# Fused attention and feed-forward: one more block product a span in two levels of Strassen, and the attention's last multiply at the end of its run

## The chip, the cores and the metric

The kernel runs on one core of a Trainium2 chip. The metric is the device time of one execution in microseconds (us); the time of a kernel is the median of several executions. The core's engines are PE (matrix multiply; PEld is its weight load), DVE (vector), ACT (scalar and activation functions), POOL (the general engine) and SP, whose queue issues most of the DMAs here. Each engine takes its instructions strictly in the order in which the program wrote them, so work that waits on one engine holds back everything written behind it on that engine.

## The reference, cut to what matters

```python
batch, n_heads, seq, head_dim = (8, 12, 448, 64)
n_tokens, d_model, d_ff = (3584, 768, 2048)

q_n, k_n = (rmsnorm(q, g_q), rmsnorm(k, g_k))
scores = np.matmul(q_n, k_n.transpose(0, 1, 3, 2)) / np.sqrt(head_dim)
attn = np.exp(scores - np.max(scores, axis=-1, keepdims=True))
attn = attn / (np.sum(attn, axis=-1, keepdims=True) + 1e-09)
x = np.matmul(attn, v)            # then (B,H,S,D) -> (B*S, H*D)

h = x @ w_in                      # 3584 x 768 by 768 x 2048
g = np.maximum(h, 0.0) ** 2
out = g @ w_out                   # 3584 x 2048 by 2048 x 768
```

All is in float32. An x column is scaled by one over the sum of its exponentials; the kernel keeps the sum apart from the product with v and multiplies at the end. These are the "factors" of this text.

## The kernel before

The eight batches are taken two at a time, in four spans. A span holds 2 x 448 tokens and 12 head pairs (two heads side by side fill 128 partitions). Two batches side by side are what makes both feed-forward products 2 x 2 block problems, and each of these is done with Strassen's method in Winograd's form, seven block products in place of eight, named A11, A12, S1, S2, S3, A22, S4 after the weight block or sum that each takes. The weights' blocks and sums are worked out once, in the first stretch of the program, and stored in DRAM (`w1s`, `w2s`), from which they stream through five buffers (`sw`).

The order of the work is written out by hand. First the attention of span 0 alone (`attention_alone`). Then for each span: its first product (`first_product`: x by w_in, ReLU, square, and the differences of g that the second product needs), and then its second product (`second_product`: g by w_out) woven into the attention of the next span (`attention`). The last span's second product is done by `last_product`, which the change does not touch.

**The weaving.** `attention(first)` is a generator that stops (`yield`) five times a head pair, 66 times in all, and between two stops the main loop (L1497 to L1500) takes some steps of `second_product`, one step being one matmul of a filling product (PE runs it as two instructions). The attention of a head pair leaves at its first stop one solid block on PE (scores of the chunks 0 and 1, values of the pair before, scores of the chunks 3 and 2), and then PE has only filling until the next pair's block.

**A head pair on the other engines.** ACT: exponentials (L794), a copy of half of the values (L1004), four small copies for the norm (L748), the scaling of the transposed q (L769), the squares for the pair after next (L738), three small copies of the folded sums (L827). DVE: the sums of exponentials (L817, L815), the norm's reduction (L745) and arithmetic (L755, L756), transposes of the next pair (L768), the join of the two halves of the values (L910), x times its factors (L912), the folding of the sums (L824) and the factors themselves (L834 to L836). POOL: the power of -1/2 (L757), the norm's multiplies (L759), the combinations of x for the first product's Strassen sums in the second batch of a span (L922 to L927), a small DMA of the factors to DRAM (L1031), and two DMAs (L842) that read them back spread over 64 partitions each, straight into x's place, where L912 multiplies.

**The second product.** `FIRST[span]` of the seven block products are done in one level, as filling: three blocks of 8 matmuls of 448 columns each, every block evicted by DVE (L1195, L1197) or ACT (L1192), and those that complete an output are transposed on DVE (L1257) and stored by four DMAs (L1260). The others come after, in two levels: of their three row blocks, two are split again (28 matmuls of 224 columns for the parts pa, pb, pc, pd), and the third is done as before (`ps`, L1219). Their weights come as a set of four quarters (`load_set`, L1138), POOL adds up the weight sums (L1150, L1151, L1211, L1212), and DVE the sums of g (`add_g`, L1145). Which dead parts of the big buffers gT and gC hold the sets, the sums and the outputs is written out at the head of `second_product`. In the attention beside span 0's second product DVE also has the differences of g to do (`combine`, L1043 to L1047), as span 0's first product does not do them.

`FIRST` is (6, 5, 5): one product in two levels in span 0, two each in spans 1 and 2.

Of the kernel before, what the change touches and what calls it, by code (L numbers as in the profile page):

```python
# [387 lines left out]
def attention_then_ffn_bounded(  # L388
# [258 lines left out]
    FIRST = (6,5,5)  # L647
    order2 = (A11, A12, S2, S1, S3, A22, S4)
    plan, begins = [], {}
    for span in range(NSPAN):  # L650
# [3 lines left out]
        if span + 1 < NSPAN:  # L654
            plan += [(w2s[i, k, :, :, m * P:(m + 1) * P], 2 * NFC) for o, i in enumerate(order2)
                     for m in range(HC) if o < FIRST[span] or m == HC - 1 for k in range(HF // 4)]

# [232 lines left out]

    def finish(i):

        b, hp = divmod(i, NPAIR)
        pav, factors = pavs.pop(i), xT[:, b % 2, hp]
        x = factors
        if i < NAT:

# [10 lines left out]
        else:  # L908
            rest = rests.pop(i)
            nc.vector.tensor_tensor(rest, pav, rest, ALU.add)  # L910
            pav = rest
# [72 lines left out]
    def attention(first):  # L984
# [3 lines left out]
        for i in range(first, last + 1):  # L988
# [30 lines left out]
            if i > first:  # L1019
                finish(i - 1)  # L1020
# [5 lines left out]
            if i > first:  # L1026
                combine_x(i - 1)
            yield
            if i < last:
                factors_of(i)  # L1030
                nc.gpsimd.dma_start(sums["out"][i % 2], sums["square"][0:2 * S // 32, 1])  # L1031
                spread(i)
            yield
# [72 lines left out]
    def second_product(work, span):  # L1106
# [3 lines left out]
                  A12: gT[:, HF:, 0:S], A22: gC[:, 2], S4: gT[:, HF:, S:2 * S]}  # L1110
        HK, HS, NB = HF // 2, S // 2, HF // 2 * P
# [3 lines left out]
        first, end = FIRST[span], len(order2)  # L1115
# [3 lines left out]
        zone = {end - k: gC[:, k - 1].rearrange("p f n -> p (f n)") for k in (1, 2)}  # L1119
        tiles = {o: [z[:, k * NB:(k + 1) * NB].rearrange("p (c m) -> p c m", c=HK) for k in range(6)]  # L1120
                 for o, z in zone.items()}
        p1s = [work.tile([P, S], F32, tag="p1", name="p1", bufs=HC) for _ in range(HC)]
        ys = [work.tile([P, S], F32, tag="y", name="y", bufs=1)] + [zone[end - k][:, 6 * NB:6 * NB + S] for k in (2, 1)]
        spared = [gT[:, f, S:2 * S] for f in range(HF)]
        squares_of = [gT[:, HF + k, 0:S].rearrange("p (g n) -> p g n", n=32) for k in range(5)]

        def t_of(o, k):
            rows = gT[:, o % 2 * HF + 2 * k:o % 2 * HF + 2 * k + 2, 0:S]
            return rows.rearrange("p r (h n) -> p r h n", h=2)

        def parts_of(o):
            rhs = rhs_of[order2[o]]
            return [[rhs[:, k * HK:(k + 1) * HK, t * HS:(t + 1) * HS] for t in range(2)] for k in range(2)]

        def load_set(o):
            if o < end:
                for k, (m, h) in enumerate(((0, 0), (0, 1), (1, 0), (1, 1))):
                    nc.sync.dma_start(tiles[o][k], w2s[order2[o], h, :, :, m * P:(m + 1) * P])  # L1138
# [14 lines left out]
        def send(o):  # L1153
            for k in range(len(late)):
# [453 lines left out]
```

## Time and profile before

| | us |
|---|---|
| three executions: median (lowest, highest) | 1349.33 (1349.3, 1349.94) |
| the profiled execution, its own time | 1347.0 |
| its span, first to last instruction | 1345.2 |

| stage (us from the span's start) | length | DVE busy | ACT busy | POOL busy |
|---|---|---|---|---|
| 262.0 to 436.0, attention beside span 0's second product | 174.0 | 140.91 | 77.49 | 102.77 |
| 436.0 to 456.0, its two-level product | 20.0 | 8.61 | 0.56 | 8.38 |
| 581.5 to 737.0, attention beside span 1's second product | 155.5 | 119.98 | 75.85 | 101.80 |
| 737.0 to 776.0, its two two-level products | 39.0 | 20.52 | 1.36 | 18.23 |
| 900.0 to 1055.0, attention beside span 2's second product | 155.0 | 119.79 | 75.69 | 101.82 |

PE is busy in all of these from end to end, and the granted clock is 1.00 in each. A time of a kernel is that of the whole execution; the span is a little shorter, since something lies ahead of the first and behind the last recorded instruction. In rows of the profile "line engine op, out<-in" stands for a group of instructions or for a single one; in a timeline a row begins with the start and the length, and a bracket at its end says how long the engine had been idle before and which instruction's end let it go.

### The profile page before, as it was taken

To read this page: it belongs to the slowest core of one execution; us is meant where nothing else is said; L and a number is where in the kernel's file an instruction comes from. 1 tells how busy PE (TensorE), PEld (TensorE's weight loads), DVE (VectorE), ACT (ScalarE), POOL (GpSimd) and SP (SyncE) were. 2 spreads that over 40 slices of the span, in tenths; PEclk is the share of its full clock that TensorE was granted. 3 is DMA by queue.
4 is the path that set the end of the run, shared out by engine and by line. 5 is a ranking of instruction groups with operands and counts; after the bars stand their busy time and mean duration, and the time that the engine had idled before them with its cause. 6 is when DMAs were issued, how large, how long until landed. Compare 5 with 4: busy or idle time off the path is not lost.

```text
span 1345.2 us, 17641 instructions
## 1 busy us (share of the span) xinstructions
PE 1324.3 (98%) x5906; PEld 694.3 (52%) x5906; DVE 841.6 (63%) x1325; ACT 485.4 (36%) x938; POOL 664.2 (49%) x539
## 2 busy tenths in 40 slices
PE   8999999999999999999999999999999999999997
PEld 3333445444444655444444755444444665556887
DVE  6999788589777333467877523357777723336553
ACT  7886466544543011345553011235554101111000
POOL 5766533466574322647675412447676522322452
PEclk9999999999999999999999999999999999999999
DMA  8967999655666333345757333345664534421433
GB/s 226 249 210 201 315 361 328 186 130 118 132 131 157 90 88 88 98 109 125 152 128 168 79 96 88 91 114 118 128 130 125 127 89 135 133 87 50 115 102 58
DMA packets 413818, 190.19 MB, mean 141 GB/s; under 512 B 282388, under 2 KB 408724, under 8 KB 413716
## 3 DMA queue, kind: packets, MB, share of 16 engines
q1 hardware_dynamic: 406164, 180.21, 51.4%
q0 software_dynamic: 4736, 8.40, 2.4%
q8 instruction: 49, 0.80, 0.2%
q10 hardware_dynamic: 2816, 0.34, 0.2%
q14 instruction: 53, 0.43, 0.1%
HBM read 155.72 MB, written 33.16 MB: 140 GB/s over the span
## 4 chain that ended last, share of the span: by engine, by line
PE 87%; DVE 7%; ACT 3%; issue 1%; DMA 0%; SPq 0%; POOL 0%; ACTq 0%; DVEq 0%
PE ps L1175 21%; PE pd L1083 11%; PE pa L1083 10%; PE pc L1083 10%; PE sc L792 7%; PE pav L874 6%; PE pb L1083 5%; PE ps L1352 3%; PE ps L1219 2%; PE pd L1324 2%; PE pa L1324 2%; PE pc L1324 2%; ACT gT L804 1%; DVE gT L817 1%; PE pc L1160 1%
## 5 line engine op out<-in xcount | busy, mean ns | idle before, releaser
L757 POOL TENSOR_TENSOR half<-half,mhalf 128x28 f32<-128x28 f32 x36 | 184.5, 5125 | 83.6 <-DVE half L756 73.2
L1059 POOL TENSOR_TENSOR gT<-gT 128x448 f32<-128x448 f32 x96 | 93.8, 978 | 258.5 <-ACT gT L1055 258.5
L1175 PE MATMUL ps<-gT,sw 128*128 128x448 f32 x432 | 169.3, 545 | 0.0
L1055 ACT ACTIVATE gT<-gT 128x448 f32<-128x448 f32 x96 | 55.4, 577 | 300.1 <-DVE gT L1098 297.8
L1083 PE MATMUL pa<-xT,sw 128*128 128x448 f32 x384 | 155.0, 540 | 0.6 <-ACT p L1087 0.6
L1175 PE MATMUL ps<-gC,sw 128*128 128x448 f32 x336 | 131.4, 545 | 0.0
L1175 PEld LDWEIGHTS ps<-gT,sw 128*128 128x128 f32 x432 | 80.1, 190 | 87.5 <-issue 85.5
L792 PE MATMUL sc<-qkT 64*64 64x448 f32 (+1 forms) x1152 | 110.3, 497 | 0.3 <-ACT pr L794 0.2
L1083 PEld LDWEIGHTS pa<-xT,sw 128*128 128x128 f32 x384 | 72.7, 190 | 71.6 <-issue 70.3
L583 POOL TENSOR_TENSOR gC<-gC 128x384 f32<-128x384 f32 x64 | 76.4, 1211 | 63.1 <-DVE gC L579 61.4
L1175 PEld LDWEIGHTS ps<-gC,sw 128*128 128x128 f32 x336 | 62.4, 190 | 68.1 <-issue 66.1
L794 ACT ACTIVATE pr<-sc 128x896 f32<-128x896 f32 x87 | 76.8, 908 | 11.7 <-PE sc L792 11.7
L1098 DVE TENSOR_TENSOR gT<-z,pd 128x448 f32<-128x448 f32 x32 | 19.8, 619 | 97.7 <-PE pd L1083 82.0
L842 POOL DMA_DIRECT2D xT<-factors x72 | 38.0, 532 | 84.1 <-DMA factors<-square 60.0
L1083 PE MATMUL pd<-xT,sw 128*128 128x448 f32 x192 | 77.9, 542 | 1.5 <-DVE z L1090 1.3
L1083 PE MATMUL pd<-xC,sw 128*128 128x448 f32 x192 | 77.5, 540 | 0.7 <-DVE gT L1098 0.7
L1083 PE MATMUL pb<-xC,sw 128*128 128x448 f32 x192 | 77.5, 540 | 0.1
L1083 PE MATMUL pc<-xC,sw 128*128 128x448 f32 x192 | 77.4, 539 | 0.0
L1083 PE MATMUL pc<-xT,sw 128*128 128x448 f32 x192 | 77.4, 539 | 0.0
L874 PE MATMUL rest<-pr,vt 64*64 64x448 f32 x348 | 72.7, 537 | 0.0
L874 PE MATMUL pav<-pr,vt 64*64 64x448 f32 x348 | 72.7, 537 | 0.0
L759 POOL TENSOR_TENSOR qk<-qk,half 128x448 f32<-128x448 f32 x72 | 69.9, 991 | 2.8
(276 smaller groups left out, 2387.8 us busy)
## 6 DMA issues: line engine op xcount, KB each, us to landing
sw<-w1s SPq DMA_DIRECT2D x224, 192.0 KB, 2.4
sw<-w2s SPq DMA_DIRECT2D x106, 256.0 KB, 3.5
w1s<-gC SPq DMA_DIRECT2D x8, 1344.0 KB, 6.9
w2s<-gC SPq DMA_DIRECT2D x8, 1344.0 KB, 6.1
qk<-in_q_dram SPq DMA_DIRECT2D x144, 56.0 KB, 2.6
qk<-in_k_dram SPq DMA_DIRECT2D x144, 56.0 KB, 2.5
xT<-factors POOLq DMA_DIRECT2D x72, 112.0 KB, 3.6
out_dram<-osb SPq DMA_DIRECT2D x124, 56.0 KB, 1.9
```

Source lines behind the costliest of these rows:

```text
L583: nc.gpsimd.tensor_tensor(*[blocks_of(n)[:, place_of(n, i)] for i in (dst, x, y)], op)
L757: nc.gpsimd.tensor_tensor(half, half, mhalf, ALU.pow)
L759: nc.gpsimd.tensor_tensor(qkn[:, s], raw[:, s], half[:, s * NG:(s + 1) * NG].rearrange("p g -> p g ()").to_broadcast([P, NG, 32]), ALU.mult)
L792: nc.tensor.matmul(sc[part, h, 0:n], qkT[rows, 0, 1, keys], qkT[rows, 0, 0, of], start=True, stop=True)
L794: nc.scalar.activation(pr, sc[:, :, 0:n], AF.Exp)
L874: nc.tensor.matmul(into, vs[i][rows, h, c, :], probs[i, c][rows, h, :], start=(c == 0), stop=(c == NF), skip_group_check=True)
L1055: nc.scalar.activation(g, src, AF.Relu)
L1059: nc.gpsimd.tensor_tensor(g, g, g, ALU.mult)
L1083: nc.tensor.matmul(ps, stream[n + at][:, c], rhs[:, c], start=first and c == 0, stop=c == HC - 1, skip_group_check=not first)
L1175: nc.tensor.matmul(ps, stream[n][:, c % 4], rhs_of[i][:, c], start=c == 0, stop=c == HF - 1)
L1324: nc.tensor.matmul(ps, lhs[:, c], rhs[:, c], start=first and c == 0, stop=c == HK - 1, skip_group_check=not first)
L1352: nc.tensor.matmul(ps, weights_of(o, m, c // HK)[:, c % HK], rhs_of[i][:, c, part], start=c == 0, stop=c == HF - 1)
```

## The change

`FIRST` becomes (5, 4, 4): two products in two levels in span 0, three each in spans 1 and 2. Where it is 4, the order of the seven products is another one, so that A12 falls among the three, and S2 plus S1's running sums get tiles of their own (`zs`) beside `p1s`.

In the attention, the old `finish` is cut in two. `join` (the addition of the two halves of the values, which frees their PSUM bank) stays in its place; the multiply with the factors, and behind it `combine_x`, move to the end of the pair's run, behind the two DMAs of the next factors.

In span 0 the differences of g are spread over more of the filling. The four sums of g for the first two-level product are done one at a time, a block apart; each later set of weights is loaded one product ahead, and the weight sums for it are added later in the product. The sets, sums and outputs of the two-level products have new places, among them the attention's tiles of exponentials. The line-order change in the main loop moves only where the generator object is made.

```diff
-    FIRST = (6,5,5)
-    order2 = (A11, A12, S2, S1, S3, A22, S4)
+    FIRST = (5,4,4)
+
+    def order2(span):
+
+        return (A11, S2, S1, S3, A12, A22, S4) if FIRST[span] == 4 else (A11, A12, S2, S1, S3, A22, S4)
...
+    def join(i):
+
+        rest = rests[i]
+        nc.vector.tensor_tensor(rest, pavs.pop(i), rest, ALU.add)
+
     def finish(i):
...
         else:
-            rest = rests.pop(i)
-            nc.vector.tensor_tensor(rest, pav, rest, ALU.add)
-            pav = rest
+            pav = rests.pop(i)
         nc.vector.tensor_tensor(x, pav, factors, ALU.mult)
...
             if i > first:
-                finish(i - 1)
+                join(i - 1)
             if i + 3 < last:
                 squares(i + 3)
             yield
             if i < last:
                 fold(i)
-            if i > first:
-                combine_x(i - 1)
             yield
             if i < last:
                 factors_of(i)
                 nc.gpsimd.dma_start(sums["out"][i % 2], sums["square"][0:2 * S // 32, 1])
                 spread(i)
+            if i > first:
+                finish(i - 1)
+                combine_x(i - 1)
             yield
...
-        zone = {end - k: gC[:, k - 1].rearrange("p f n -> p (f n)") for k in (1, 2)}
-        tiles = {o: [z[:, k * NB:(k + 1) * NB].rearrange("p (c m) -> p c m", c=HK) for k in range(6)]
-                 for o, z in zone.items()}
...
+        zone = [gC[:, k].rearrange("p f n -> p (f n)") for k in range(2)]
+        tiles = {o: [zone[(first + 1 - o) % 2][:, k * NB:(k + 1) * NB].rearrange("p (c m) -> p c m", c=HK)
+                     for k in range(6)] for o in range(first, end)}
+        b11, b21, b12 = ([gT[:, r + f, at:at + S] for f in range(HF)] for r, at in ((0, 0), (HF, 0), (0, S)))
+        apart = first == 4
+        exps = [pr[:, h] for pr in places[:NJ] for h in range(2)]
+        homes = {first: exps, first + 1: b21 if apart else b12, first + 2: b12}
...
-                        if span == 0 and at < 8 * HF and at % 4 == 1:
-                            combine(at // 4 % HF, (at // 4 // HF,))
+                        if span == 0 and at < 6 * HF and at % 6 == 1:
+                            combine(at // 6, (0,))
+                        if span == 0 and 6 * HF <= at < 11 * HF and at % 5 == 4:
+                            combine(at // 5 - 9, (1,))
                         if c == 3:
-                            send(o)
-                        if o == first - 1 and c == 5:
-                            if m < 2:
-                                load_set(first + m)
-                            for k in ((0, 1), (2,), (3,))[m]:
-                                add_g(first, k)
-                            if m == 2:
+                            send()
+                        ahead = (o - first + 1) * HC + m + 1
+                        if ahead >= 0 and c == 5:
+                            if ahead == 1:
+                                load_set(first)
+                            add_g(first, ahead)
+                            if ahead == HC:
                                 add_weights(first)
...
             for k in range(3):
                 add_g(o + 1, k)
-            send(o)
+            send()
+            load_set(o + 1)
             ps = bank("ps")
...
             nc.vector.tensor_tensor(y, z, pc, add)
-            add_weights(o + 1)
-            deliver(work, span, third, HC - 1 + where[0], where[1],
-                    osb=rows_of[3].rearrange("p (g n) -> p g n", n=32))
+            deliver(work, span, third, HC - 1 + col, t, osb=home[4].rearrange("p (g n) -> p g n", n=32))
...
             nc.vector.tensor_tensor(into[1][:, left], into[1][:, left], pd, add)
+            add_weights(o + 1)
```

## The prediction

> **What bounds the kernel now.** I read the page first (engines, then the chain that ended last), then the chain in order of time, then the timelines of PE, DVE, ACT and POOL around one attention pair.
>
> ```profile
> PE 1324.3 (98%) x5906; PEld 694.3 (52%) x5906; DVE 841.6 (63%) x1325; ACT 485.4 (36%) x938; POOL 664.2 (49%) x539
> PE 87%; DVE 7%; ACT 3%; issue 1%; DMA 0%; SPq 0%; POOL 0%; ACTq 0%; DVEq 0%
> ```
>
> PE is busy throughout and carries the chain. So the first thing to ask of the change is how much less PE streams. The chain at the end of span 1's attention gives the price of a two-level product and of a block of a one-level one, and an earlier piece gives the place of one attention pair (the stretch of filling matmuls between two blocks of scores and values):
>
> ```profile
> 651.15 6.96 PE ps L1175 x18
> ...
> 742.21 1.51 PE pa L1160 x8
> 743.72 6.01 PE ps L1219 x16
> ...
> 758.81 1.51 PE pa L1160 x8
> ```
>
> A full block (16 instructions) takes 6.01 us, so a one-level product of three blocks takes 18.03. A two-level product takes 758.81 - 742.21 = 16.60. In between PE never stops, so PE alone sets that pace.
>
> Next I looked for what holds PE when it does stop. There is one clear place, in span 0, where the ACT and the PE timelines read
>
> ```profile
> 335.36 0.69 ACT L827 COPY quarters<-quarters 32x28 f32<-32x28 f32 x3 [2.77 <-DVE quarters L824]
> ```
>
> ```profile
> 337.70 0.98 PE L792 MATMUL sc<-qkT 64*64 64x448 f32 x8 [0.19 <-ACT pr L794]
> ```
>
> ACT works in order. Its small copies of DVE's column sums (L827, for pair i) stand ahead of the exponentials of pair i+1, and PE needs those to free the two score banks. The block of scores there began at 332.47 and the next filling at 338.61: 6.14 us, against 5.43 for an undisturbed block (683.57 to 689.00). So 0.71 us were lost because L827 began 2.89 us after the block did. The allowance is therefore 2.89 - 0.71 = 2.18 us after a block's start. What leads to L827 is DVE's row of work for a pair, here the pair whose filling began at 651.15:
>
> ```profile
> 651.31 1.16 DVE L768 STREAM_TRANSPOSE qkT<-qk 128x448 f32<-128x448 f32 x2
> 653.58 0.19 DVE L755 TENSOR_TENSOR half<-half,other 128x28 f32<-128x28 f32 x1 [1.11 <-ACT other L748]
> 653.80 0.18 DVE L756 TENSOR_SCALAR half<-half 128x28 f32<-128x28 f32 x1
> 653.98 0.65 DVE L1257 STREAM_TRANSPOSE osb<-ct 128x448 f32<-128x448 f32 x1
> 654.55 1.05 DVE L817 TENSOR_TENSOR acc<-acc,qkT 128x896 f32<-128x896 f32 x1
> 655.63 1.27 DVE L815 TENSOR_TENSOR acc<-acc,half 64x448 f32<-64x448 f32 x2
> 656.93 0.62 DVE L910 TENSOR_TENSOR half<-pav,half 128x448 f32<-128x448 f32 x1
> 657.59 0.62 DVE L912 TENSOR_TENSOR xT<-half,xT 128x448 f32<-128x448 f32 x1
> 658.13 1.10 DVE L824 TRANSPOSE_TENSOR_REDUCE quarters<-acc 128x28 f32<-128x896 f32 x1
> ```
>
> L824 ends 8.08 us after the filling began, though the block started at 658.11: only 1 us of allowance is left. And POOL, for the same pair, works round a loop of its own:
>
> ```profile
> 654.13 4.82 POOL L757 TENSOR_TENSOR half<-half,mhalf 128x28 f32<-128x28 f32 x1 [1.06 <-DVE half L756]
> 659.03 1.84 POOL L759 TENSOR_TENSOR qk<-qk,half 128x448 f32<-128x448 f32 x2
> 661.27 0.60 POOL L1031 DMA_DIRECT2D factors<-square  x1 [0.39 <-DVE square L836]
> 665.26 1.05 POOL L842 DMA_DIRECT2D xT<-factors  x2 [3.40 <-DMA factors<-square]
> ```
>
> It stands still between its two DMAs until the first has landed.
>
> **The sum, on PE.** Three products change from 18.03 to 16.60 us: 3 x 1.43 = 4.29 us less. That is the whole of what the change can give by doing less.
>
> **What is taken from under the attention.** Spans 1 and 2 now fill twelve pairs with 4 x 24 - 6 = 90 matmul steps where there were 114, spread over 61 turns, five a pair: 7.38 steps of 0.751 us (6.01 / 8) = 5.54 us a pair instead of 7.02. The pair's period, 12.62 us in span 1 (fillings begin at 600.84 and, ten pairs on, at 726.99), becomes 11.14. Span 0 goes from 14.2 to 12.62. DVE, ACT and POOL have the same attention to do in that shorter time.
>
> **DVE's row, spans 1 and 2.** L755 starts 2.43 us after the filling begins, since it waits for ACT's copies behind the exponentials, and this stays. From there: 0.40 to the end of L756, 1.08 (L817), 1.30 (L815), 0.66 (L910), 1.10 (L824): 6.97. The change takes L912 out of this row (0.54, and its wait for the spread DMA: 13.5 us in 13 places over the kernel), and the output transpose L1257 (0.57) is in no pair before S3. With 0.1 for the semaphore L827 starts at 7.07; the allowance is 5.54 + 2.18 = 7.72 (7 or 8 steps: 7.44 to 8.19). Margin 0.65. Into it come the evictions that the filling puts between (L1195, 0.56: S2's and S1's, about one in five pairs of the twelve, 0 to 0.2 lost each, 0.3 in all), and in one pair a g-sum of the second level as well (L1145, 1.05 to 1.91): 7.07 + 0.56 + 1.25 = 8.88 against 8.19, 0.7 lost. I take 1.0 a span. Bounds: 0 if the evictions fall into DVE's wait for ACT's copies, 3.8 if POOL sets the pace (below).
>
> **POOL's loop.** Its nine rounds in span 1 (592.10 to 703.90, without its waits for DVE and ACT) add up to 103.6 us, 11.5 each; in span 2 to 102.4. Against 11.14 it falls 0.36 us behind per pair, 3.2 us by the tenth, or 2.2 since PE's own loss of 1.0 gives it time. In the pair above the normalised tile was ready at 660.87 and its transpose started at 663.68, 2.8 us of reserve; the shorter period takes 1.48, and the 1.3 us by which L768 may slip before L755 is late come to it: 2.6. So it just holds, by 0.4 us.
>
> **Span 0.** The subtractions L1043 to L1047 (0.63 to 0.76 each) were two every 4 steps, and are now two every 6 and then every 5, one such pair of them inside DVE's row: 7.07 + 1.3 + an eviction of 0.56 to 1.13 = 8.9 to 9.5, against 7.02 + 2.18 = 9.2 (8.9 to 9.7). Four or five pairs lose 0 to 0.5: 1.6 us, where 0.71 was lost before. Net 0.9; bounds -0.7 and 2.5.
>
> **Into the first two-level product.** POOL's weight sums (L1150, L1151) stand behind the last run's spread and now behind three x combinations too (L925 to L927), which before ran while POOL waited. From the end of L836: 0.55 + 2.0 + 1.05, then 4.2, 2.65 and 1.35 (L1211): 11.8. L836 ends about 8.5 us after the last filling began, so a11 is ready at 20.3; PE wants it after 5.54 + 2.79 (values) + 4.51 (six steps) + 7.52 (pa and third block) = 20.4. I take 0.2 for each of spans 1 and 2, bounds 0 and 1.5; span 0 has 1.5 us more filling and costs nothing.
>
> **What I cost at nothing.** The tile set of the second and third two-level product is loaded one product ahead, behind 4 or 8 output DMAs on SP's queue (0.48 each) and their transposes: it starts 9 us into a product, needs 2.65 to issue and 4.7 to land (gC<-w2s), 14.3 of 16.6; if late, the next pa waits, 1 us each. Separate S2+S1 sums (zs), new homes for the outputs and the moved sums of g add no instruction. The exponential of the half chunk (L794) now waits for the later L912, 9.3 us after the filling began at the earliest, and its scores come at 10.5; behind it stand the exponential of chunk 2 and L1004.
>
> [...] L1145 took from 1.04 to 2.15 us for one and the same shape, and POOL's L925 1.13 or 1.92. [...]
>
> **Sum.** 4.29 - 0.9 (span 0) - 2.0 (two attention runs) - 0.4 (two entries) = 1.0 us. The profiled execution would go from a span of 1345.2 (1347.0 with what lies around it) to 1344.2 (1346.0). The median shown, 1349.33, is 2.33 above it, so 1348.3.
>
> **Rivals.** *The loops hold everywhere:* L912's waits were what made DVE late, and no pair loses PE time. For it: PE does not stop in spans 1 and 2 now. Against: 0.65 us of margin. Then 4.29 + 0.71 = 5.0, 1344.3; with half of my 3.3 us of losses 1346.7. *POOL becomes the bound:* each wait for the factors' landing took 1.33 to 3.88 us (mean 2.3). If it is 2.65 in the denser traffic, POOL's rounds add 9 x 0.35 = 3.2 us a span, 2.8 beyond the 0.4 left, 5.6 in two: 1.0 - 5.6 = -4.6, 1353.9. It decides from a mean of about 2.35, with 1.8 us for each further 0.1. Against: bytes per us stay the same, as the loads of filling weights go with the filling. *The wait is only moved:* L912 at the end of a run holds ACT at the half chunk, then chunk 2 and DVE's L817; at 0.25 us in each of twenty pairs that is 5 us against the 1.0, 1353.3. Against: 1.2 us of cover.
>
> **How the numbers follow.** 0.2% is 2.7 us, about what a measurement of this kernel can tell from no change. My sum lies within it: 0.42. Faster by more (1346.6 or less) needs losses under 1.6 us: 0.32. POOL's loop 0.17 and the moved wait 0.09 make slower 0.26. The range leaves out the very fastest and the far part of the slow cases: 1345.0 to 1353.0; the likeliest case alone is 1346.6 to 1351.
>
> **What would show it.** Two-level products 16.6 us apart, three in a row in spans 1 and 2. Waits of PE's score loads on ACT's exponentials of 0.1 to 0.7 us, mostly in the pairs with S1 and S3. POOL's idle time before L757 near zero from the second pair on. L912 with no wait for the spread. Wrong: gaps of over 1 us in each pair (POOL or the half chunk sets the pace), pb waiting for L1211 by over 1 us, or pa waiting for its tile set.

## The result, and the profile after

The changed kernel takes 1364.60 us (1361.09 to 1367.10), the one before 1349.32 beside it: 1.0106 of its time, 95% interval 1.0086 to 1.0125. The forecast was 1348.3, within 1345 to 1353. It was wrong in sign: 15 us slower instead of 1 us faster. The profiled execution took 1367.1 us with a span of 1365.3, so it is at the upper end of the runs.

Engines and chain of the changed kernel's page:

```profile
PE 1329.1 (97%) x5978; PEld 706.0 (52%) x5978; DVE 881.5 (65%) x1349; ACT 485.6 (36%) x941; POOL 699.6 (51%) x560
PE 68%; DVE 10%; POOL 7%; ACT 5%; issue 4%; DMA 4%; SPq 1%; POOLq 0%; ACTq 0%; DVEq 0%
```

PE had 87% of the chain and has 68%; DVE, POOL, ACT, issue and DMA have the rest. DVE is 40 us busier and POOL 35, for 24 and 21 instructions more, which take 1.3 us or less each where nothing stands beside them. So instructions that were there before take longer. What PE waited for (us in total, times, longest):

```profile
PE pb L1174 <- POOL gC L1232: 4.9, 3, 2.3
PE sc L796 <- ACT pr L798: 4.7, 17, 0.7
...
PE pav L878 <- DVE half L898: 1.6, 2, 1.0
```

The first of them is the way into each run of two-level products, the others lie in the attention pairs. By stage, from the starts of PE's first matmul in each (the third column is the stage before, less 18.03 us for each one-level product taken out, or 16.6 for each two-level product):

| stage, us | before | PE's work after | after | lost |
|---|---|---|---|---|
| attention of span 0 | 177.08 | 159.05 | 159.18 | 0.1 |
| two-level products, span 0 | 16.61 | 33.2 | 34.00 | 0.8 |
| attention of span 1 | 158.33 | 140.30 | 148.15 | 7.85 |
| two-level products, span 1 | 33.22 | 49.8 | 52.09 | 2.3 |
| attention of span 2 | 158.56 | 140.53 | 146.92 | 6.4 |
| two-level products, span 2 | 33.21 | 49.8 | 54.12 | 4.3 |

That is 21.8 us lost against a gain of 4.29, 17.5 net. The two profiled spans differ by 20.1; the other 2.6 us lie ahead of the first of these stages and behind the last, where the change does nothing. What happens in a pair is seen where POOL's two norm multiplies (L763; L759 before) stand beside DVE's row. The timeline of the kernel before, round the end of a row (start, duration, engine, line):

```profile
672.13 1.84 POOL L759 TENSOR_TENSOR qk<-qk,half 128x448 f32<-128x448 f32 x2
...
673.03 0.20 DVE L836 STREAM_TRANSPOSE square<-square 32x32 f32<-32x32 f32 x1
...
674.02 1.09 DVE L817 TENSOR_TENSOR acc<-pr,qkT 128x896 f32<-128x896 f32 x1 [0.78 <-ACT qkT L794]
```

and the same pair of the changed kernel:

```profile
669.03 2.22 POOL L763 TENSOR_TENSOR qk<-qk,half 128x448 f32<-128x448 f32 x2
...
669.47 0.20 DVE L840 STREAM_TRANSPOSE square<-square 32x32 f32<-32x32 f32 x1
669.61 0.84 DVE L919 TENSOR_TENSOR xT<-half,xT 128x448 f32<-128x448 f32 x1
...
670.37 1.82 DVE L821 TENSOR_TENSOR acc<-pr,qkT 128x896 f32<-128x896 f32 x1
```

Before, the multiplies run beside DVE's three small instructions (the last, L836, is shown) and end as the addition that follows (L817) begins, which takes 1.09 us. After, they reach into L919 (0.84 instead of 0.57) and the addition (L821, 1.82 instead of 1.09), and are stretched themselves. In spans 1 and 2 of the changed kernel all 20 pairs of multiplies overlap L919 or L821; before, 7 of 20 touched L817, four of these by 0.03 us or less.

As a measure I take, from each trace, DVE's two-input instructions (TENSOR_TENSOR) that begin in the attention stages of spans 1 and 2, and add up what each took above the shortest of its shape there, where that is over 0.15 us. Before it is 5.6 us, after 22.5.

### The profile page after: what moved, and what is told of

Same layout as the page of the kernel before. It is cut to its first block, busy times and chain, and to the rows that moved or that the text cites. A ratio compares the mean times of both kernels' runs of the same rounds, so it can differ in the third digit from the quotient of the medians.

```text
span 1365.3 us, 17930 instructions
## 1 busy us (share of the span) xinstructions
PE 1329.1 (97%) x5978; PEld 706.0 (52%) x5978; DVE 881.5 (65%) x1349; ACT 485.6 (36%) x941; POOL 699.6 (51%) x560
## 4 chain that ended last, share of the span: by engine, by line
PE 68%; DVE 10%; POOL 7%; ACT 5%; issue 4%; DMA 4%; SPq 1%; POOLq 0%; ACTq 0%; DVEq 0%
PE pd L1091 10%; PE pa L1091 10%; PE pc L1091 10%; PE ps L1189 8%; PE pb L1091 5%; PE sc L796 3%; PE ps L1372 3%; PE pav L878 3%; POOL half L761 3%; PE ps L1241 2%; PE pc L1174 2%; PE pd L1174 2%; PE pd L1344 2%; ACT gT L808 2%; PE pa L1344 2%
## 5 line engine op out<-in xcount | busy, mean ns | idle before, releaser
L1189 PE MATMUL ps<-gT,sw 128*128 128x448 f32 x336 | 133.2, 546 | 0.0
L796 PE MATMUL sc<-qkT 64*64 64x448 f32 (+1 forms) x1152 | 114.2, 501 | 6.7 <-ACT pr L798 4.7
L1189 PE MATMUL ps<-gC,sw 128*128 128x448 f32 x288 | 113.4, 546 | 0.0
L1189 PEld LDWEIGHTS ps<-gT,sw 128*128 128x128 f32 x336 | 61.9, 190 | 69.3 <-issue 68.6
L1189 PEld LDWEIGHTS ps<-gC,sw 128*128 128x128 f32 x288 | 53.2, 190 | 59.5 <-issue 58.8
L763 POOL TENSOR_TENSOR qk<-qk,half 128x448 f32<-128x448 f32 x72 | 77.6, 1098 | 2.8
```

The costliest lines, as they stand in the source:

```text
L763: nc.gpsimd.tensor_tensor(qkn[:, s], raw[:, s], half[:, s * NG:(s + 1) * NG].rearrange("p g -> p g ()").to_broadcast([P, NG, 32]), ALU.mult)
L796: nc.tensor.matmul(sc[part, h, 0:n], qkT[rows, 0, 1, keys], qkT[rows, 0, 0, of], start=True, stop=True)
L1189: nc.tensor.matmul(ps, stream[n][:, c % 4], rhs_of[i][:, c], start=c == 0, stop=c == HF - 1)
```

## The experiments

Theory after the result: DVE's row sets the pace, and it is lengthened where POOL's multiplies, combinations and weight sums coincide with DVE's two-input instructions; and POOL stands before pb at the entry. First rival: POOL's own round, 11.5 us in a pair of 11.14, sets the pace. Line numbers of variants differ from the changed kernel's by a few. The table gives all twelve; "stretch" is the measure above. They were taken at several times and on several chips, on which the kernel before took 1348.0 to 1350.0, so differences between rows are worked out from the ratios, times 1349.3.

| run | us | ratio to before, 95% interval | attention 1, 2 | two-level 1, 2 | stretch |
|---|---|---|---|---|---|
| changed kernel | 1364.60 | 1.0106 [1.0086, 1.0125] | 148.15, 146.92 | 52.09, 54.12 | 22.5 |
| e1_555 | 1349.87 | 0.9999 [0.9989, 1.0009] | 158.33, 158.33 | 33.53, 33.45 | 13.3 |
| e2_cheap_power | 1371.17 | 1.0154 [1.0137, 1.0171] | 149.21, 146.65 | 53.95, 54.32 | 27.5 |
| e3_hide_wait | 1376.81 | 1.0203 [1.0177, 1.0230] | 150.61, 151.42 | 50.55, 54.21 | 39.5 |
| e4_old_finish | 1369.18 | 1.0139 [1.0119, 1.0158] | 153.50, 150.04 | 49.82, 50.06 | 3.1 |
| e5_gate_cheap | 1353.87 | 1.0037 [1.0027, 1.0047] | 141.93, 141.94 | 52.42, 54.31 | 8.8 |
| e6_small_sp | 1351.03 | 1.0020 [1.0010, 1.0030] | 143.01, 143.50 | 50.85, 52.07 | 15.9 |
| e7_weights_early | 1358.82 | 1.0071 [1.0053, 1.0088] | 147.31, 146.36 | 49.82, 49.82 | 21.5 |
| e8_sp_early | 1350.55 | 1.0013 [1.0003, 1.0023] | 145.71, 144.37 | 49.82, 49.82 | 21.0 |
| c1_sp_reduce | 1348.82 | 1.0004 [0.9995, 1.0014] | 141.31, 142.20 | 50.89, 52.08 | 12.5 |
| c3_sp_reduce_gated | 1350.94 | 1.0018 [1.0008, 1.0028] | 144.57, 144.78 | 49.83, 49.82 | 19.6 |
| c5_gated | 1346.44 | 0.9991 [0.9982, 1.0000] | 141.51, 142.96 | 49.82, 49.82 | 8.9 |
| c6_gated_555 | 1344.32 | 0.9973 [0.9964, 0.9983] | 158.33, 158.34 | 33.21, 33.21 | 7.8 |

**Which of the three products costs the time.** One number changed:

```diff
-    FIRST = (5,4,4)
+    FIRST = (5,5,5)
```

> FIRST is (5, 5, 5): all of the change but the two products taken from under the attention of spans 1 and 2. Both theories, that POOL's round or that DVE's row became longer than PE's pair there, put the loss into those two spans, so the time comes back to 1347 to 1350 us, and the attention stages of spans 1 and 2 to about 158.3 us without stops of PE. If the loss were in what moved (the late multiply, the new places, span 0's spread differences), it would stay above 1355.

All of the loss is gone: the product taken in span 0 loses nothing in its attention (158.95 us), the pairs of spans 1 and 2 are back at 12.6 us. The stretch of 13.3 us costs nothing there, since the row has the room. The loss is that of the third two-level product in spans 1 and 2.

**Is it POOL's round?** Two ways to give POOL time. The first replaces the power of 5.1 us by a subtraction, which leaves the norm out:

```diff
-        nc.gpsimd.tensor_tensor(half, half, mhalf, ALU.pow)
+        nc.gpsimd.tensor_tensor(half, half, mhalf, ALU.subtract)
```

> The changed kernel with POOL's power (L761, 5.1 us a pair) replaced by a subtraction of the same tile, so the norm is left out. Theory POOL (its round of 11.6 us without a gap sets the pace of 11.14): PE's stops in the attention of spans 1 and 2, 6 to 8 us each in the changed kernel, shrink to under 2 us each; time 1347 to 1351. Theory DVE (its row up to the fold, with the evictions, sets the pace): POOL gets 40 per cent idle and the time stays above 1358.

The second keeps the power, and puts the multiplies between the two DMAs, where POOL stood still:

```diff
                 nc.gpsimd.dma_start(sums["out"][i % 2], sums["square"][0:2 * S // 32, 1])
+                if i + 2 < last:
+                    scale_rows(i + 2)
                 spread(i)
```

> The changed kernel with POOL's order changed: the norm's two multiplies (2.3 us) stand between the small DMA of the factors and the DMAs that read them back, where POOL waited 2.2 us for the landing. Nothing is left out. Theory POOL: the round falls from 11.6 to about 9.5 us, under PE's 11.14, and the time to 1348 to 1353. Theory DVE: no gain, above 1358.

Both are slower than the changed kernel, by some 6.5 and 13 us: with time to spare on POOL the kernel lost more. So a long round of POOL isn't needed for a loss of this size. Whether it counts in the changed kernel itself is another question, since both edits also moved the multiplies; it is taken up below. The timeline of e2_cheap_power shows what costs the time there:

```profile
652.61 1.08 DVE L821 TENSOR_TENSOR acc<-acc,qkT 128x896 f32<-128x896 f32 x1
652.63 3.13 POOL L763 TENSOR_TENSOR qk<-qk,half 128x448 f32<-128x448 f32 x2
653.72 2.53 DVE L819 TENSOR_TENSOR acc<-acc,half 64x448 f32<-64x448 f32 x2
```

The earlier multiplies now stand beside the two half-chunk additions L819: those take 2.53 us instead of 1.27, the multiplies 3.13 instead of 1.84. In e3_hide_wait they stand beside the first addition (there L829), and in 19 rounds of 20 it is stretched:

```profile
663.70 3.02 DVE L829 TENSOR_TENSOR acc<-pr 128x896 f32<-128x896 f32 x1 [0.17 <-ACT pr L806]
...
663.91 1.84 POOL L771 TENSOR_TENSOR qk<-qk,half 128x448 f32<-128x448 f32 x2
```

DVE began first and yet ended 0.97 us after both multiplies: it had nearly all of its 1.09 us still to do when POOL had done. Each of these rounds gets up to 1.9 us longer on DVE, and PE waits behind it (e3_hide_wait, PE's waits):

```profile
PE pav L886 <- DVE half L906: 6.4, 12, 0.8
PE sc L804 <- ACT pr L806: 6.0, 26, 1.4
```

**What POOL's late multiplies hold up in the changed kernel.** The changed kernel's own trace shows a second way, which neither theory named. SP loads the q and k of a later pair into the buffer that POOL's multiplies read, so each load waits for a multiply's end. SP's waits for this in span 1, before and after (us in total, times, longest):

```profile
SPq L684 <- POOL qk L759: 23.1, 7, 4.8
SPq L688 <- POOL qk L763: 40.7, 10, 7.5
```

ACT squares what was loaded (L742), and in ACT's order these squares stand ahead of the copies of the folded sums (L831). A pair of span 2, from the timelines of POOL, SP, ACT and DVE:

```profile
949.02 2.43 POOL L763 TENSOR_TENSOR qk<-qk,half 128x448 f32<-128x448 f32 x2
...
950.58 1.90 SPq L688 DMA_DIRECT2D qk<-in_q_dram  x4
952.58 2.13 SPq L688 DMA_DIRECT2D qk<-in_k_dram  x4
...
955.66 1.10 DVE L828 TRANSPOSE_TENSOR_REDUCE quarters<-acc 128x28 f32<-128x896 f32 x1
...
957.81 0.95 ACT L742 ACTIVATE qk<-qk 128x896 f32<-128x896 f32 x1 [4.21 <-DMA qk<-in_k_dram]
958.78 0.69 ACT L831 COPY quarters<-quarters 32x28 f32<-32x28 f32 x3
```

The load of q begins as the first of the two multiplies ends. The block of scores began at 955.34. DVE's row ended at 956.76, in time, but the copies began only at 958.78, and the block lost 1.27 us. So it went in five blocks of the two runs, 6.4 us of their 14.2. In the other blocks that lost time the copies begin within 0.1 us of L828's end, and DVE's row sets the time: some 8 us, of which 5.9 in four pairs (the last two with a power in each span) where L919 is stretched, in two of them L821 too, and L759, 0.14 to 0.19 us elsewhere, takes 1.2 to 1.6 beside POOL's L929. In e2_cheap_power and e5_gate_cheap (below) no block waits for squares.

**Was the late multiply by the factors a mistake?** finish and combine_x put back into their old places:

```diff
                 join(i - 1)
+                finish(i - 1)
...
             if i < last:
                 fold(i)
+            if i > first:
+                combine_x(i - 1)
...
-            if i > first:
-                finish(i - 1)
-                combine_x(i - 1)
```

> The changed kernel with x times its factors and the combinations of x back in their old places, ahead of the fold and of the small DMA. Both theories: DVE's row grows by 0.55 us and the wait for the spread DMA in each pair, and POOL's small DMA comes later by as much, so 5 to 12 us slower than the changed kernel: 1369 to 1377. If the late multiply had been what costs the time (it holds ACT at the half chunk), this would be faster than the changed kernel, 1352 to 1360.

No: without it the kernel is some 4.5 us slower still (the two intervals overlap a little; the attention stages, 153.50 and 150.04 us, are clear). DVE's groups of e4_old_finish in span 1 (busy, mean ns | idle before, and what ended it):

```profile
L819 DVE TENSOR_TENSOR acc<-acc,half 64x448 f32<-64x448 f32 x24 | 14.9, 620 | 0.8
...
L919 DVE TENSOR_TENSOR xT<-half,xT 128x448 f32<-128x448 f32 x11 | 6.9, 625 | 9.9 <-DMA xT<-factors 9.4 <-DVE half L898 0.3
```

Little is stretched here, but the row waits 9.4 us for the landing of the factors instead (1.9 in the changed kernel). That is a second way in which the row gets too long, and the change was right to remove it. It has a price, though: with the multiply and the x combinations in their old places the entries are free (49.82 and 50.06 us), so it is their move to the end of the run that put POOL's combinations ahead of the weight sums.

**The same work at another place.** e2_cheap_power once more, with the multiplies held until L819 has ended, by a copy of one element on POOL:

```diff
                 add_up(i, 2)
                 add_up(i, 3)
+            if i + 2 < last:
+                nc.gpsimd.tensor_copy(sums["mark"], sums["acc"][0:1, 0, 0:1])
+                scale_rows(i + 2)
```

The expectations from here on call it a lock when POOL's and DVE's instructions stretch each other; what is measured of it so far are the 2.53 and 3.13 us of e2_cheap_power and the 3.02 of e3_hide_wait above.

> Same work as e2_cheap_power (the power replaced by a subtraction, so the norm is left out of the result), and POOL's two norm multiplies are held back until DVE's half-chunk addition L819 has ended, so that they run beside L898, the fold L828 and L838 to L840. Theory of the lock (a DVE instruction with two SBUF inputs and a POOL instruction that reads SBUF hold each other up): the two L819 cost 1.27 us together again instead of 2.5, the two multiplies 1.84 instead of 2.6 to 3.1, pairs of spans 1 and 2 come at about 11.1 us, the time falls from 1371.2 to 1350 to 1356. Rival, DVE's row is too long even without any lock: the durations become right but the period stays at 11.8 or more and the time at 1362 or more. Second rival, POOL's own loop sets the pace: no gain over 1371, since POOL now starts its multiplies later.

```profile
648.87 1.27 DVE L827 TENSOR_TENSOR acc<-acc,half 64x448 f32<-64x448 f32 x2
...
649.61 0.56 POOL L1036 COPY mark<-acc 1x1 f32<-1x1 f32 x1 [1.92 <-DVE acc L827]
650.14 1.83 POOL L771 TENSOR_TENSOR qk<-qk,half 128x448 f32<-128x448 f32 x2
650.17 0.62 DVE L907 TENSOR_TENSOR half<-pav,half 128x448 f32<-128x448 f32 x1
650.71 1.10 DVE L836 TRANSPOSE_TENSOR_REDUCE quarters<-acc 128x28 f32<-128x896 f32 x1
```

One small instruction more per pair, a later start of the multiplies, and 15.8 us less. The multiplies run beside L907 (one input from PSUM) and L836 (one input), and nobody is stretched: 1.83, 0.62 and 1.10 us. Attention takes 141.9 us against 140.4 of PE's work. So what the place of the multiplies costs is shown with the work the same, in a kernel whose POOL has time to spare. The wait of pb stays (5.5 us in three places, two-level products 52.42 and 54.31).

**The real kernel: give POOL's round room.** With the power at its full 5.1 us the multiplies can't come that early. What can be had is the small transfer's issue:

```diff
-                nc.gpsimd.dma_start(sums["out"][i % 2], sums["square"][0:2 * S // 32, 1])
+                nc.sync.dma_start(sums["out"][i % 2], sums["square"][0:2 * S // 32, 1])
```

> Changed kernel with the small transfer L1036 of the reciprocals issued by SP instead of POOL (result unchanged). POOL's round falls from 0.6 + 2.4 + 1.05 + 5.1 + 1.84 = 11.0 to 11.5 us to some 8 us of work with the landing wait in parallel, so that the power starts at a fixed distance behind L840 and the multiplies end about when the next L840 ends. Theory (POOL's round without reserve lets the multiplies slide into L919 and L821, where the lock holds both up): collisions with L821 get rare, 4 to 10 us less than the changed kernel, 1355 to 1361. Rival, DVE's row alone is too long: 1364 within 2. Rival against the edit: SP waits for L840 with block loads behind it, PE waits for DMA, over 1367.

11.6 us less than the changed kernel, more than expected. The transfer no longer waits behind the multiplies, so the power starts earlier against DVE's row, and 10 of the 20 multiplies in spans 1 and 2 stay clear of L821, where 5 did. No load of weights came late: PE's waits for them are 0.3 us in all.

**The entry.** The set of the first two-level product is loaded earlier, and its two weight sums stand one block earlier:

```diff
-                        if ahead >= 0 and c == 5:
-                            if ahead == 1:
+                        if ahead >= -1 and c == 5:
+                            if ahead == -1:
                                 load_set(first)
-                            add_g(first, ahead)
-                            if ahead == HC:
+                            else:
+                                add_g(first, ahead)
+                            if ahead == 2:
                                 add_weights(first)
```

> Changed kernel with the first two-level product's weight set loaded two filling products of 22 steps earlier and its two weight sums on POOL one earlier, so that they are not in a row with the x combinations at the end of the run (result unchanged). Theory (the stop of pb behind POOL costs 0.5, 2.0 and 2.3 us, and the one of span 2 brings 3.4 us of half clock, some 1.4 us more): pb waits under 0.5 us, no half clock behind it, 4 to 6 us less than the changed kernel, 1359 to 1361. Rival: the sums only meet DVE's row one pair earlier, 1364 within 2.

> Both edits of e6_small_sp and e7_weights_early (result unchanged). Theory: the gains add, 8 to 16 us less than the changed kernel, 1349 to 1356. If one of them has no effect alone, the time is that of the other.

Alone it brings 4.7 us, as expected: 49.82 us in both spans, which is PE's work. Together with e6_small_sp it brings only 0.5: the entry's 3.3 us are had, but the attention takes 2.7 and 0.9 us more. The time lies in the expected range, but not for the expected reason: the gains don't add (12.5 us together, 11.6 and 4.7 alone).

**A better place for the sum of squares, and held weight sums.** c1_sp_reduce is e6_small_sp with L749, which has one input (1.07 to 1.08 us in ten places of the changed kernel where it runs beside the multiplies), right behind L840, where late multiplies meet it instead of L919 and L821:

```diff
                 nc.sync.dma_start(sums["out"][i % 2], sums["square"][0:2 * S // 32, 1])
+                if i + 3 < last:
+                    reduce_squares(i + 3)
                 spread(i)
...
+            if i + 2 < last:
+                if i == first:
+                    reduce_squares(i + 2)
+                swap_halves(i + 2)
...
-            if i + 2 < last:
-                norm_by_squares(i + 2)
```

> e6_small_sp with DVE's sum of squares L749 (one input, so outside the lock) moved from behind the first L821 to just behind L840, and ACT's swap L752 ahead of its copy of the rest (result unchanged). In e6_small_sp 11 of the 20 multiplies of spans 1 and 2 still run into L919 and L821 and stretch the pair's two by 0.7 to 1.2 us; their attention takes 143.0 and 143.5 us against 140.4 of PE's work. Theory of the lock: with L749 in that place the multiplies meet an unlocked instruction, and the power starts up to 1 us earlier; collisions with L821 fall to a few, attention of spans 1 and 2 to 141 to 142.5, the time from 1351.0 to 1347 to 1350. Rival: the wait for the swapped halves on ACT still sets the start of the power, or L821 now starts later by L749's 1.07 us and the row is no shorter: 1350 to 1353.

As the theory said: 141.31 and 142.20 us, and the time is that of the kernel before. c3_sp_reduce_gated adds the weight sums, one in each of the last two rounds behind a copy as in e5_gate_cheap, and the load of e7_weights_early:

```diff
+            if last - 2 <= i < last and "weights" in sums:
+                nc.gpsimd.tensor_copy(sums["mark"], sums["acc"][0:1, 0, 0:1])
+                sums["weights"]()
```

> c1_sp_reduce, and the two weight sums of the first two-level product, each behind the end of L819 in one of the last two rounds, beside L898, L828 and L838 to L840 (result unchanged). In e8_sp_early the same sums, taken out of the entry without a choice of place, left the two-level products at 49.82 us (PE's work) but cost 2.7 and 0.9 us in the rows that they met. Theory of the lock: entry free and rows undisturbed, two-level products 49.8 us, attention as in c1_sp_reduce, 2 to 3.5 us less than that, 1344 to 1347, under the kernel before. Rival: the rows of the last rounds are lengthened all the same by DVE's combinations L1159, time within 1 us of c1_sp_reduce.

2.1 us more instead of 2 to 3.5 less. The sums themselves are not stretched (1.26 us each), so neither side had the cause. Its POOL timeline shows it:

```profile
691.39 1.12 POOL L853 DMA_DIRECT2D xT<-factors  x2 [4.48 <-DMA factors<-square]
...
693.62 5.23 POOL L768 TENSOR_TENSOR half<-half,mhalf 128x28 f32<-128x28 f32 x1
698.93 2.88 POOL L770 TENSOR_TENSOR qk<-qk,half 128x448 f32<-128x448 f32 x2
```

The early set (four loads of 256 KB on SP's queue, issued from 682.92 on) stands ahead of the small transfer (686.39). POOL waits 4.48 us for its landing; in c1_sp_reduce, where the set comes later, it waits 0.48 at this place. The last power starts late, its multiplies meet L927 and the addition, and the x combinations that follow meet L828 and the half-chunk additions. So c5_gated loads the set one block later than that (behind the small transfer that the last power's round waits for), does both sums in the last round but one, and holds the last x combinations in the same way:

```diff
+            if i >= last - 2:
+                if i < last:
+                    nc.gpsimd.tensor_copy(sums["mark"], sums["acc"][0:1, 0, 0:1])
+                if i == last - 2:
+                    sums.pop("weights")()
+                else:
+                    combine_x(i - 2)
...
-                combine_x(i - 1)
+                if not last - 2 <= i < last:
+                    combine_x(i - 1)
```

> c1_sp_reduce, with the first two-level product's set loaded one step (8 filling matmuls) earlier, its two weight sums on POOL behind L819's end in the last round but one (where POOL has no power left), and the x combinations of the last two rounds behind L819's end of the following round instead of beside L821 and L819 (result unchanged). In c1_sp_reduce the two-level products of spans 1 and 2 take 50.89 and 52.08 us against 49.82. Theory: entry free, 49.82 both, attention 141 to 142.5 as in c1_sp_reduce, 2.5 to 4 us less than that: 1345 to 1346.5, 0.1 to 0.25% under the kernel before. Rival, as in c3_sp_reduce_gated: the rows of the last two rounds are lengthened by what was taken from the entry, time 1348 to 1351.

> The same edits with FIRST = (5,5,5), that is with span 0's two-level product taken and the third ones of spans 1 and 2 given back (result unchanged). Its pairs of spans 1 and 2 come every 12.6 us, so that neither POOL's round nor the lock has anything to lengthen. Theory: the third two-level product is worth its 1.4 us a span once the multiplies no longer collide, so this kernel takes 2 to 3 us more than c5_gated, 1348 to 1349.5, near e1_555 (1349.9). Rival: the fourth product taken from beside the attention costs as much as it brings even without collisions, both kernels within 1 us.

c5_gated's time, 0.9991 of the kernel before with an interval that reaches 1.0000, is at the upper end of what was expected. Its entries are free as the theory said, but against c1_sp_reduce it gains 1.8 us by the ratios, not 2.5 to 4, and the attention of span 2 takes 142.96 us. c6_gated_555 is not where it was expected: with the third two-level products of spans 1 and 2 given back it takes 2.1 us less than c5_gated, not 2 to 3 more, and 0.9973 of the kernel before. Its interval lies below the kernel before and below the changed one. PE has 82% of the chain of c5_gated and 89% of that of c6_gated_555.

Even with the collisions placed as well as I could, a pair of 11.14 us has residues (141.51 and 142.96 us where PE's work is 140.30 and 140.53, 3.6 in all) that eat the 2.9 us of the two products. Some 2.6 of the 3.6 us aren't collisions: they are lost in four blocks whose copies stand behind squares that waited 3.9 to 4.6 us for their loads. The expectation that the third product pays once the multiplies no longer collide left this out. In c6_gated_555's stages 1.5 us of its gain of 3.6 on the kernel before are to be seen: span 0's attention and two-level products together take 192.16 us, before 193.69. The other 2 us are in no stage of its one profiled execution, which was the slowest of its nine; where they come from stays open.

## Why the prediction was wrong

**PE's gain** was right. 16.6 us each is what c5_gated's three two-level products take (49.82), and with nothing in the way pairs come at the predicted period: e5_gate_cheap's fillings begin at 599.3 and, ten pairs on, at 712.2, 11.29 us against 11.14.

**DVE's row** is the first of two steps that failed. It went "From there: 0.40 to the end of L756, 1.08 (L817), 1.30 (L815), ..." with the shortest durations of the kernel before, and took L755's start 2.43 us behind the filling as given: "and this stays". In pairs that nothing disturbs it holds: L828 ended 6.8 to 6.9 us behind the filling in the first two pairs of span 1 (predicted 6.97). In the next six it was 7.5 to 8.7, and L755's counterpart (L759) began up to 1.0 us later than 2.43. In four of the six the first addition, ahead of the row's part that I added up, was stretched (in two of them L919 too), in one L919 and L759, and in one an eviction (L1216) with its wait for PE stood ahead of the transposes. Evictions stood in the row itself in four of the six, where I had allowed for one pair in five. That one and the same addition can take twice its time was known from L1145, 1.04 to 2.15 us. One more such stretch a pair, 1.1 us against 0.65 of margin, is 9 us in twenty pairs and makes 1357 of the forecast, an estimate from these rows; that is still 7.6 us short, but of the right sign. I kept to the shortest durations because L1145's mean, 1.37, is only 0.3 above its shortest. The mean was the wrong row to take: it is that of another instruction, in a kernel with 12.6 us a pair, in which POOL's multiplies fell on DVE's small instructions in most pairs. Here collisions weren't spread at random over the loop; they followed its phase, and the change moved the phase (7 of 20 pairs of multiplies touched the first addition before, all 20 touch L919 or L821 after). The loss in the two attention runs was put at 2.0 and is 14.2, some 8 of it by DVE's row. The allowance that the row was held against was right: behind the first block of each run, what a block lost is the start of L831 after the block's, less 2.18 us, to within 0.03.

**POOL's loop**, "it just holds, by 0.4 us", is the second. The rounds were read rightly: 11.5 us each, and from 605.40 to 651.36 five powers of the changed kernel start 11.5 us apart with no idle time ahead of them. But the reserve was taken at one place only, the transposes that wait for the normalised tile. The same multiplies free the buffer for the next loads of q and k, ACT's squares wait for these, and the copies stand behind the squares: 6.4 us in five pairs, a path that the sum doesn't have. Being out of reserve also moved the multiplies, from the end of DVE's small instructions into L919 and L821. The rival in which POOL's landing wait sets the pace had its condition unmet (2.2 us each in ten landings of span 1 and 2.0 in ten of span 2, where it needed over 2.35); POOL was late without it. e6_small_sp, which shortens the round, wins in both ways: the blocks behind squares lose 3.2 us there and the others 2.5. No run changes one of the two alone in the real kernel, so their shares rest on the traces.

**The entry** was mis-sized: 0.2 us each with bounds of 0 and 1.5, nothing in span 0; measured 2.3, 4.3 and 0.8. The working had the weight sums at 2.65 us and a11 ready 0.1 us early. In the changed kernel's timeline at the end of span 2 both engines are stretched:

```profile
1060.39 6.18 PE L1241 MATMUL ps<-gT,sw 128*128 128x448 f32 x16
1061.12 1.97 POOL L934 TENSOR_TENSOR xT<-xT 128x448 f32<-128x448 f32 x1
1063.06 2.11 POOL L1164 TENSOR_TENSOR gC<-gC 128x512 f32<-128x512 f32 x1
1065.25 2.00 POOL L1165 TENSOR_TENSOR gC<-gC 128x512 f32<-128x512 f32 x1
...
1067.33 1.52 POOL L1232 TENSOR_TENSOR gC<-gC 128x512 f32<-128x512 f32 x1
...
1068.91 2.12 PE L1174 MATMUL pb<-gT,gC 128*128 128x224 f32 x8 [2.34 <-POOL gC L1232]
```

L1164 and L1165 took 4.11 us instead of 2.65, while DVE's three sums L1159 beside L934 to L1165 took 1.43, 1.90 and 2.15 instead of 1.05 each. That is the stretch of both sides at a second place. The rest of span 2's 4.3 us is told in the last section.

**Span 0** was put at a net loss of 0.9; its attention lost 0.1. Four or five pairs were to lose 1.6 us, and one lost 0.22, where 0.71 had been lost before. The subtractions that I put into the row cost PE next to nothing. This step was wrong by 0.8 us on the cautious side.

**Costed at nothing** was right in what it named. No pa waited for its tile set, and the half chunk's wait for the later multiply isn't what costs the time: e4_old_finish, without that wait, is slower, since the row then waits for the factors. The loads of q and k, which did cost, aren't among what it named. That the multiply in its new place waits little for the spread was right too (1.9 us in span 1, 5.1 before).

**What of the lock.** The theory behind the expectations took in every POOL instruction that reads SBUF. The runs bear it out for POOL's multiplies, combinations and weight sums: L819 went from 1.27 to 2.53 us and the two multiplies beside it from 1.84 to 3.13 (e2_cheap_power), and the first addition from 1.09 to 3.02 beside the multiplies (e3_hide_wait). In the changed kernel L759, 0.14 to 0.19 us elsewhere, takes up to 1.56 beside the combination L929, and the weight sums 4.11 instead of 2.65 at the entry of span 2. DVE's single-input and PSUM-reading instructions kept their time: 1.10 and 0.62 us beside the multiplies in e5_gate_cheap, and 0.62 (L898) in six places beside the combinations in the changed kernel. The runs don't bear it out for POOL's power, as the last section shows. What in the hardware does this isn't shown.

## What to carry to other kernels

When a loop is packed closer, don't price its contention by a mean over the old loop: write out, for the new period, which instruction of one engine stands beside which of the other, and add what your own traces show where two of them meet. Here a two-input DVE instruction beside POOL's multiplies, combinations or sums took up to the whole of that work on top (1.9 us for 1.84 in e3_hide_wait); beside the power there was nothing to add (0.62 us with it and without). When an engine falls behind, follow everything that its instructions release, buffers for later loads too, and not only the next reader. An engine that has just enough time in a loop has no hold on its phase; a small piece of work moved off it (0.6 us in e6_small_sp, 11.6 gained) or a held start can be worth more than the work that the change saved. And take the gain apart by stage before keeping a change: here the product in span 0 lost next to nothing in its attention, and the other two lost more than they brought.

## What the runs showed of the hardware

**Half the clock behind five of nine stops of PE.** In span 2 PE's third block ended at 1066.57 and pb began at 1068.91, a stop of 2.34 us. From there the changed kernel's stretches read (busy time of each engine, granted clock, DMA share and GB/s):

```profile
1066.00:1070.00 4.00, 1.66 (x8) 1.10 (x7) 3.86 (x5) 0.00 (x0) 3.84 (x3) 1.00 0.34 58
1070.00:1074.00 4.00, 4.00 (x14) 3.68 (x13) 2.38 (x5) 0.00 (x0) 1.73 (x3) 0.57 0.81 229
```

The mean granted clock was 0.57 from 1070 to 1074 and 0.50 from 1071 to 1073; if all of the reduction was to 0.50, it held for 3.4 of the 4 us. pc's eight matmuls took 3.07 us where pd's took 1.68, about 1.4 us more, and pb's 2.12. The same followed the stops of pb of 2.18 and 2.55 us in e2_cheap_power, 2.44 in e3_hide_wait and 2.54 in e5_gate_cheap (granted clock 0.57 to 0.60 over 4 us), but not the one of 2.34 us in span 1 of e5_gate_cheap, nor those of 2.0 us in span 1 of the changed kernel and in span 2 of e6_small_sp and c1_sp_reduce, whose stages lost the stop and 0.3 us. The stages of the other five lost the stop and some 1.95 us. So the lower clock followed stops of 2.18 to 2.55 us in five cases of six, and stops of 2.0 us in none of three; what decides it isn't shown.

**Which of the two waits.** In e3_hide_wait DVE's addition was mostly 0.21 us old as POOL's first multiply began, and in 19 of the 20 rounds POOL ran both multiplies at full speed and DVE took the whole delay. In the round at 1005.39 DVE was as old, and there the addition kept its 1.09 us and the multiplies took 2.58. POOL's issue of the small transfer (0.58 us) was under way when the addition began in the one round as in the others like it, so it doesn't tell them apart. In e2_cheap_power, where multiplies and additions followed each other on both sides, both were stretched (2.53 and 3.13 us). By the order of the starts in these traces it can't be told which side is held up.

**POOL's power held nobody up.** In the kernel before, 40 half-chunk additions and 8 additions of 128x896 in spans 1 and 2 lie wholly within a power (L757, 4.8 to 5.5 us). They took 0.62 and 1.05 to 1.09 us, as without it; the rows of the prediction show one such pair at 654.13. In the changed kernel it is the same (21 of 0.62 us, 4 of 1.08 to 1.13). So here not every POOL instruction with inputs in SBUF stretched DVE's.

**A transfer of 3.5 KB that landed late.** With the set of 1 MB issued on SP ahead of it (from 682.92 on, the small transfer of the reciprocals at 686.39) POOL waited 4.48 us for the landing, without it 0.48 (c3_sp_reduce_gated and c1_sp_reduce at the same place). That the queue made it wait behind the set is the nearest reading; no run shows where the time went.
